# Attention with two folded feed-forward blocks: half-wide last transposes, products in 512-token blocks, and a new list of priorities

## The chip, the cores and the metric

The kernel runs on one core of one Trainium2 chip. A core has five engines with a queue each: TensorE (PE) multiplies matrices, VectorE (DVE), ScalarE (ACT) and GpSimd (POOL) work element by element, SyncE (SP) issues transfers. The metric is the device time of one execution in microseconds (us); less is better. The kernel before takes 956.4 us, the median of three runs from 956.32 to 956.83.

## The reference

```python
# q, k, v: (4, 8, 576, 64); s: (4, 8, 576); float32 throughout
scores = q @ k.T / 8
cum = cumsum(max(s, 0))
scores = where(causal, -1e9, scores + min(-(cum[i] - cum[j]), 0))
p = exp(scores - max(scores))
p = p / (sum(p) + 1e-09)
x = (p @ v).transpose(0, 2, 1, 3).reshape(2304, 512)
x = ((x @ w1) * (x @ w2)) @ w3 @ w_out     # 512 -> 1024 -> 1024 -> 512
h = x @ w_in                               # 512 -> 2048
out = (h - tanh(h)) @ w_out2               # 2048 -> 512
```

There are 32 heads (4 batches of 8), 576 tokens each.

## The kernel before

Every float32 product is made of three: a number is split into a high part (the rounded value, a cast) and a low part (the rest, a subtraction), and high x high, low x high and high x low are added up in one bank of the accumulator memory PSUM (eight banks of 128 x 512 float32, bank 58 to 65 in the orders below).

*Attention.* A head has five query tiles (64, 128, 128, 128, 128 queries). For each, PE multiplies the scores (lines 644 to 650; in batch 0, the "full" heads, one float32 product with the bias in extra rows of the operands, later two products of split operands), DVE adds the mask and takes the maximum in one pass (line 660), ACT takes the exponential with its sum (line 666). PE transposes the result e in blocks of 128 keys (`flip`, line 698), one engine copies it to SBUF as en, and PE multiplies by v for two heads together (line 730). For such a pair of heads `inverses` adds 1e-9 to the sums on DVE (line 676), takes the reciprocal (line 677), transposes it on PE (line 678), writes it to DRAM and reads it back broadcast; the result xf is multiplied by it (line 760, DVE or POOL) and split into xh and xl. Two heads give one of the four quarters k of the 512 columns of x.

*Products.* `products(j)` takes 384 tokens: for each of 8 column blocks f of w1 and w2 it adds up 4 quarters x 3 matmuls for a in bank 64, the same for b in bank 65 (line 782), copies a to SBUF (asb), multiplies b by it (line 789) and stores c. The quarters' last one can be multiplied only when the last two heads of a batch have passed the whole chain above. The weights come in as raw 64-bit pieces and are converted: absolute value on ACT (line 487), four passes on DVE (lines 488 to 493), a cast (line 389 on ACT or 390 on DVE) and a subtraction (394 or 395).

*Behind attention.* wa = w3 @ w_out, folded once (lines 838 to 840); x2 = c @ wa (lines 876 to 878); h = x2 @ w_in (line 915); g = h - tanh(h) in about ten steps over ACT, DVE and POOL (lines 923 to 930, 389, 395); out = g @ w_out2 (lines 936 to 938).

*What sets the order.* The program describes all this as operations with engines, costs, buffers and priorities. A planner (`Plan`) runs through them in its own clock, gives each engine at any time the ready operation of the least priority, and chooses the engine where an operation may go on two (`copy`, `split`, `sub`; the numbers dcopy, dsub, act, pool in `PARAM` are added to that choice). The order that comes out is emitted; each engine then runs its list in order and waits by semaphores. Where the planner expects PE to wait, up to the time `fu` of its clock, it puts in a dummy 128-wide matmul (line 546).

## Time and profile before

| | |
|---|---|
| median of three runs | 956.4 us |
| profiled execution | 956.8 us |
| its span, first to last instruction | 955.1 us |
| PE busy in the span | 942.2 us, 99% |
| DVE, ACT, POOL busy | 64%, 60%, 41% |
| mean granted PE clock | 0.998 |

PE's busy time holds the dummies too, and neighbours overlap by their tails, so a mean duration is longer than the distance between two starts. A releaser is the instruction whose end let a waiting engine go on.

### The profile page before, as it was taken

What the parts mean: (1) busy time and instruction counts of PE and PEld (TensorE: products, weight loads), DVE (VectorE), ACT (ScalarE), POOL (GpSimd) and SP (SyncE); (2) the same over time, 40 slices, a digit from 0 to 9 for tenths busy, and PEclk for the clock granted to TensorE, in tenths of its full rate; (3) what the DMA queues carried; (4) which work ended last, traced back from release to release, by engine and by line L of the source; (5) the groups of instructions that cost most, each with busy time, mean ns of one, the idle gap of its engine ahead of it and who ended that gap; (6) DMA issues with size and microseconds to landing.
All of it is one profiled execution on the core that took longest, in us unless ns stands there. A gap on an engine that the chain in (4) does not pass through costs nothing.

```text
span 955.1 us, 15454 instructions
## 1 busy us (share of the span) xinstructions
PE 942.2 (99%) x5420; PEld 810.9 (85%) x5420; DVE 611.6 (64%) x1200; ACT 568.8 (60%) x1267; POOL 393.4 (41%) x323
## 2 busy tenths in 40 slices
PE   9998999999999999999999999999999999999998
PEld 7767889998889998999888888888888888888887
DVE  6996965554443399941599859986565556655644
ACT  5885656888875454431545367766555655565565
POOL 4445865446442444220888624542222222222321
PEclk9999999999999999999999999999999999999999
DMA  6654466665441255571698731231020101000010
GB/s 207 199 172 143 132 215 195 213 217 162 141 136 48 69 201 179 204 259 53 195 347 304 250 138 67 89 110 45 1 89 1 44 1 45 23 23 1 1 45 22
DMA packets 64307, 118.96 MB, mean 125 GB/s; under 512 B 6435, under 2 KB 34323, under 8 KB 64230
## 3 DMA queue, kind: packets, MB, share of 16 engines
...
HBM read 88.81 MB, written 25.46 MB: 120 GB/s over the span
## 4 chain that ended last, share of the span: by engine, by line
PE 95%; DVE 3%; ACT 1%; issue 1%; ACTq 0%; DVEq 0%
PE bank L915 21%; PE bank L782 20%; PE bank L938 7%; PE bank L936 7%; PE bank L937 7%; PE bank L698 5%; PE bank L730 5%; PE bank L876 3%; PE bank L877 3%; PE bank L878 3%; PE bank L546 2%; PE bank L647 2%; PE bank L649 2%; PE bank L650 2%; PE bank L838 2%; PE bank L840 2%
## 5 line engine op out<-in xcount | busy, mean ns | idle before, releaser
L395 POOL TENSOR_TENSOR gl<-pg,gh 128x512 fp32r<-128x512 f32 (+1 forms) x78 | 100.2, 1284 | 254.2 <-ACT gh L389 247.5
L915 PE MATMUL bank<-x2b,wih 128*128 128x512 f32 (+1 forms) x640 | 182.6, 370 | 0.0
L915 PEld LDWEIGHTS bank<-x2b,wih 128*128 128x128 f32 x640 | 116.9, 188 | 22.1
L915 PE MATMUL bank<-x2b,wil 128*128 128x512 f32 (+1 forms) x320 | 117.9, 369 | 0.0
L938 PE MATMUL bank<-voh,gl 128*128 128x512 f32 x288 | 112.9, 392 | 0.0
L936 PE MATMUL bank<-voh,gh 128*128 128x512 f32 x288 | 112.8, 392 | 0.0
L937 PE MATMUL bank<-vol,gh 128*128 128x512 f32 x288 | 112.7, 391 | 0.0
L926 DVE TENSOR_TENSOR pg<-bank,u 128x512 f32<-128x512 f32 (+1 forms) x80 | 50.4, 631 | 90.4 <-POOL gl L395 86.3
L389 ACT ACTIVATE gh<-pg 128x512 fp32r<-128x512 f32 (+1 forms) x80 | 47.0, 588 | 99.1 <-PE bank L937 96.3
L660 DVE CUSTOM_DVE_ANT_0 e<-bank,msk 128x320 f32<-128x320 f32 (+4 forms) x160 | 65.8, 425 | 61.3 <-PE bank L650 52.1
L666 ACT ACTIVATE e<-e,nmx 128x320 f32<-128x320 f32 (+4 forms) x160 | 88.9, 556 | 21.9 <-DVE nmx L660 20.9
L929 DVE TENSOR_TENSOR th<-bank,th 128x512 f32<-128x512 f32 (+1 forms) x80 | 50.8, 635 | 45.9 <-ACT th L925 45.8
L930 DVE COPY_PREDICATED pg<-mk,th 128x512 f32<-128x512 uint32 (+1 forms) x80 | 78.2, 977 | 2.5 <-ACT mk L928 0.9
L698 PE MATMUL bank<-ident,e 128*128 128x128 f32 (+1 forms) x480 | 77.0, 276 | 1.7 <-ACT e L666 0.9
L395 POOL TENSOR_TENSOR xl<-cf,xh 128x512 fp32r<-128x512 f32 (+1 forms) x40 | 54.6, 1390 | 57.7 <-ACT xh L389 57.0
L389 ACT ACTIVATE en<-bank 64x64 f32<-64x64 f32 (+3 forms) x166 | 64.3, 407 | 16.9 <-PE bank L698 15.2
L491 DVE SCALAR_TENSOR_TENSOR wt<-wraw,wt 128x512 uint32<-128x512 uint32 x72 | 73.1, 1016 | 1.2
L789 DVE TENSOR_TENSOR cst<-bank,asb 128x384 f32<-128x384 f32 x48 | 26.6, 554 | 68.9 <-PE bank L782 52.4
L782 PE MATMUL bank<-xh,w1h 128*128 128x384 f32 x192 | 69.2, 361 | 0.1
L915 PEld LDWEIGHTS bank<-x2b,wil 128*128 128x128 f32 x320 | 60.3, 188 | 10.7
L782 PE MATMUL bank<-xh,w2h 128*128 128x384 f32 x192 | 68.3, 356 | 0.0
L928 ACT ACTIVATE mk<-u,const 128x512 f32<-128x512 f32 (+1 forms) x80 | 54.1, 676 | 19.3 <-DVE pg L930 19.0
...
## 6 DMA issues: line engine op xcount, KB each, us to landing
...
```

What stands on the lines that cost most here:

```text
L389: pl.op([("ACT", c_act(n, psum), lambda: nc.scalar.activation(dst(), src(), AF.Copy)), ("DVE", c_dve(n, not psum), lambda: nc.vector.tenso ...
L395: o.append(("POOL", c_pool2(n), lambda: nc.gpsimd.tensor_tensor(dst(), a(), b().bitcast(F32), op=ALU.subtract)))
L491: dve(lambda: nc.vector.scalar_tensor_tensor(t_.t, h32(), 0xC0000000, t_.t, op0=ALU.bitwise_and, op1=ALU.bitwise_or), 512, [r_, t_], [t_], ...
L660: nc.vector.tensor_tensor_reduce(e.t[:nq, EOFF[t] + k0:EOFF[t] + k1], bk.t[:nq, :k1 - k0], bi.t[:nq, bo + k0:bo + k1], -0.125, 3.0e38 if f ...
L666: act(lambda: nc.scalar.activation(et(), et(), AF.Exp, bias=nmx.t[:nq, i, tm:tm + 1], scale=-1.0, accum_out=ssum.t[:nq, pj, t, i:i + 1]), ...
L698: nc.tensor.transpose(bk.t[:rows, n * P:(n + 1) * P], e.t[:, EOFF[t] + c * P:EOFF[t] + c * P + rows], ident.t)
L782: nc.tensor.matmul(bk.t[:, :TB], w_.t[:, k, f * P:(f + 1) * P], x_.t[:, k, o:o + TB], start=k == 0 and i == 0, stop=k == KC - 1 and i == 2)
L915: nc.tensor.matmul(bk.t[:, :w], w_.t[:, k, a], X2.t[:, i, k, :w], start=k == 0 and n == 0, stop=k == KC - 1 and n == 2)
L930: dve(lambda pg=pg, mk=mk, th=th, c_=c_: nc.vector.copy_predicated(c_(pg), c_(mk).bitcast(U32), c_(th)), w, [mk, th], [pg], pr, two=True)
L936: nc.tensor.matmul(bank[n].t, gh.t[:, a], voh[f].t, start=f == 0, stop=False)
L937: nc.tensor.matmul(bank[n].t, gh.t[:, a], vol[f].t, start=False, stop=False)
L938: nc.tensor.matmul(bank[n].t, gl.t[:, a], voh[f].t, start=False, stop=f == NF2 - 1)
```

## The change

- *Blocks of 512 tokens.* `TB` goes from 384 to 512: four blocks of 512 and one of 256 instead of six. x lies in three buffers `xb` instead of a ring over two batches. In a block a is computed for four column blocks f, then b for the same four (four asb buffers). `products(0)` is listed right behind batch 0. All pieces of w1 are converted ahead of those of w2.
- *Heads.* Batch 1's heads aren't cut in two query groups any more (`cut`), so 16 inversions of five tiles stand where 12 of five tiles, 4 of three and 4 of two stood. The full heads have three banks for scores and four for transposes until products begin. All five tiles of the first head get their bias by a product of their own (line 661 after) instead of three, and its score product is issued without waiting for the bias. The bias is centred on the tile's first key; two of the five subtractions go to ACT.
- *Half-wide transposes.* The last key block of each query tile is transposed from 64 columns only, into the last quarter of a bank. Four matmuls of zeros at the start clear that quarter (line 553 after). The tiles e are packed and their padding isn't zeroed any more; the five blocks of the last tile are copied as 3 and 2 instead of 4 and 1.
- *The 1e-9* is added by ACT (line 687 after).
- *Absolute values* of the conversions may go to DVE (line 491 after).
- *Priorities.* Nearly all numbers in `PARAM` are new; `dcopy` from 723 to -883 (copies and casts go to DVE rather than ACT), `fu` from 215.1 to 66.7 us, the conversions' `convp` from 1692.7 to 3333.5.

By engine the emitted rows go from 1202 to 1488 on DVE, from 1109 to 792 on ACT, from 328 to 309 on POOL; dummies from 370 to 117; SP's transfers from 443 to 390.

```diff
-TB = 384
-NB = NT // TB
-RING = 2 * S
+TB = 512
+NB = (NT + TB - 1) // TB
...
-PARAM = dict(cst=1050.9, ramp0=113.5, ramp1=35.9, dsub=5134.3, dsub0=979.7, dcopy=723.0, dcopy0=29.4, dother=1000.0, dother0=1000.0, spi=1234.9, lay=4, lay0=0,
...
+PARAM = dict(cst=2849.1, ramp0=-248.5, ramp1=-108.2, dsub=6619.9, dsub0=697.3, dcopy=-883.4, dcopy0=-179.8, dother=417.2, dother0=-220.2, spi=422.3, lay=4, lay0=0,
...
-    xh, xl = (xp.buf(n, [P, KC, RING], F32R, n=KC * 4) for n in ("xh", "xl"))
+    x3 = Pool("x3", "right")
+    xb = [[p_.buf(f"{n}{i}", [P, KC, TB], F32R, n=KC * 2) for n in ("xh", "xl")] for i, p_ in enumerate((xp, xp, x3))]
...
-    asb_r = abp.ring("asb", 1, [P, TB])
+    asb_r = abp.ring("asb", 4, [P, TB])
...
-        act(lambda: nc.scalar.activation(tf(), h32().bitcast(F32), AF.Abs), 512, [r_], [t_], prio)
+        pl.op([("ACT", c_act(512), lambda: nc.scalar.activation(tf(), h32().bitcast(F32), AF.Abs)),
+               ("DVE", c_dve(512, True), lambda: nc.vector.tensor_scalar(t_.t, h32(), 0x7FFFFFFF, None, op0=ALU.bitwise_and))], r=[r_], w=[t_], prio=prio, two=True, kind="copy")
...
+    def blank(b):
+        x = msk.t[:, :D].bitcast(BF16)
+        nc.tensor.matmul(b.t[:, 3 * P:], x, x, start=True, stop=True)
+    for b in bank[3:6] + bank[7:8]:
+        pe(f_mm(P), lambda b=b: blank(b), [(msk, 0)], [b], -2900)
...
+    dve(lambda: nc.vector.tensor_scalar(neg.t[2 * NH:, :5], rel.t[2 * NH:, 0:4 * P + 1:P], -1.0, None, op0=ALU.mult), 5, [(rel, 5)], [neg], -950, fast=True)
...
+        c_ = lambda x, t=t: x[2 * NH:, t * P:t * P + 1]
+        if t % 2:
+            act(lambda a=a, o=o, t=t: nc.scalar.activation(rel.t[a:a + NH, o:o + S], rel.t[2 * NH:, :S], AF.Identity, bias=neg.t[2 * NH:, t:t + 1]), S, [(rel, 5), neg], [(rel, t)], -900 + t, extra=93.0)
+        else:
+            dve(lambda a=a, o=o, c_=c_: nc.vector.tensor_scalar(rel.t[a:a + NH, o:o + S], rel.t[2 * NH:, :S], c_(rel.t), None, op0=ALU.subtract), S, [(rel, 5), neg], [(rel, t)], -900 + t, fast=True)
...
-    s_ring = Ring(bank[0:2])
+    s_ring = Ring(bank[0:2] + bank[6:7])
     pv_ring = Ring(bank[2:3])
-    tr_ring = Ring(bank[3:3 + PARAM["ntr"]])
-    ab_ring = Ring(bank[3 + PARAM["ntr"]:])
+    tr_ring = Ring(bank[3:6] + bank[7:8])
+    ab_ring = Ring(bank[6:8])
...
-            for t0, t1 in ((3, 5),) if one else ((0, 3), (3, 5)) if 1 in groups else ((0, 3),):
+            for t0, t1 in () if one and PARAM["one"] == 5 else ((3, 5),) if one else ((0, 3), (3, 5)) if 1 in groups else ((0, 3),):
...
+                    if one and t < PARAM["one"]:
                         nc.tensor.matmul(o_, rq()[:D, q0:q1], rk()[:D, k0:k1], start=True, stop=False)
-                        nc.tensor.matmul(o_, sel(a)[:, :nq], rel.t[a:a + 1, o + k0:o + k1], start=False, stop=True)
...
-                if one and t < 3:
-                    pe(2 * f_mm4(k1 - k0), mm, [(R, 0), (rel, t), (e2[1], 4)], [bk], p_)
+                if one and t < PARAM["one"]:
+                    def bias(bk=bk, k0=k0, k1=k1):
+                        a, o = ROFF[t]
+                        nc.tensor.matmul(bk.t[:nq, :k1 - k0], sel(a)[:, :nq], rel.t[a:a + 1, o + k0:o + k1], start=False, stop=True)
+                    pe(f_mm4(k1 - k0), mm, [(R, 0)], [bk], p_ - 2000.0)
+                    pe(f_mm4(k1 - k0), bias, [(rel, t), (e2[1], 4)], [bk], p_)
...
-            dve(lambda: nc.vector.tensor_scalar(sv(), sv(), 1.0e-9, None, op0=ALU.add), n, [], [(ssum, ks)], pr + PARAM["iv"])
+            act(lambda: nc.scalar.activation(sv(), sv(), AF.Identity, bias=const.t[:, 2:3]), n, [const], [(ssum, ks)], pr + PARAM["iv"], extra=93.0)
...
-            for js in [list(range(min(4, nch)))] + ([[4]] if nch > 4 else []):
+            for js in (range(nch),) if nch < 5 else (range(3), range(3, 5)):
...
+                at = 4 - n if js[-1] == nch - 1 else 0
+                half = js[-1] == nch - 1
+
+                def tr(bk=bk, js=js, at=at):
+                    for m, c in enumerate(js):
+                        rows = D if c == nch - 1 else P
+                        nc.tensor.transpose(bk.t[:rows, (at + m) * P:(at + m + 1) * P], e.t[:, EOFF[t] + c * P:EOFF[t] + c * P + rows], ident.t)
+                pe((n - half) * f_tr() + half * f_tr(D), tr, [(e, t), ident], [bk], p_)
...
+            for j in range(b * S // TB, ((b + 1) * S - 1) // TB + 1):
+                a, z, (xh, xl), p_ = max(b * S, j * TB) - j * TB, min((b + 1) * S, (j + 1) * TB) - j * TB, xb[j % 3], c * 2 + int(b * S > j * TB)
+                o = j * TB - b * S
+                split(lambda xh=xh, a=a, z=z: xh.t[:, c, a:z], (xh, p_), lambda xl=xl, a=a, z=z: xl.t[:, c, a:z], (xl, p_), lambda a=a, z=z, o=o: X.t[:, o + a:o + z], z - a, [X], pr + PARAM["ml"])
...
+        t0, t1 = j * TB, min((j + 1) * TB, NT)
+        w = t1 - t0
+        xh, xl = xb[j % 3]
+        gs = sorted({int(b * S > t0) for b in range(B) if b * S < t1 and (b + 1) * S > t0})
+        for f0 in range(0, NF, 4):
+            asb = [asb_r.next() for _ in range(4)]
+            for m, (wh, wl) in enumerate(((w1h, w1l), (w2h, w2l))):
+                for f in range(f0, f0 + 4):
+                    pos = 1.0e6 + n_prod[0]
+                    n_prod[0] += 1
+                    bk = ab_ring.next()
+                    for k in range(KC):
+                        def mm(bk=bk, wh=wh, wl=wl, f=f, k=k):
+                            for i, (w_, x_) in enumerate(((wh, xh), (wh, xl), (wl, xh))):
+                                nc.tensor.matmul(bk.t[:, :w], w_.t[:, k, f * P:(f + 1) * P], x_.t[:, k, :w],
+                                                 start=k == 0 and i == 0, stop=k == KC - 1 and i == 2)
+                        xs = [2 * k + g for g in gs]
+                        pe(3 * f_mm(w), mm, [(xh, xs), (xl, xs), (wh, k * 2 + f // 4), (wl, k * 2 + f // 4)], [bk], pos)
+                    at = asb[f - f0]
+                    if m == 0:
+                        copy(lambda at=at: at.t[:, :w], lambda bk=bk: bk.t[:, :w], w, [bk], [at], -1e6, psum=True)
+                        continue
+                    cs = cst_r.next()
+                    dve(lambda at=at, bk=bk, cs=cs: nc.vector.tensor_tensor(cs.t[:, :w], bk.t[:, :w], at.t[:, :w], op=ALU.mult), w, [bk, at], [cs], -1e6)
+                    dma(lambda f=f, cs=cs: c_d.t[:, f, t0:t1], lambda cs=cs: cs.t[:, :w], P * w * 4, [cs], [(c_d, j)], 0)
...
+        for n in range(2 * KC):
+            src, hb, lb = ((w1, w1h, w1l), (w2, w2h, w2l))[n // KC]
+            k = n % KC
+            convert(src[k * P:(k + 1) * P, half * 512:(half + 1) * 512],
+                    lambda hb=hb, k=k, half=half: hb.t[:, k, half * 512:(half + 1) * 512], (hb, k * 2 + half),
+                    lambda lb=lb, k=k, half=half: lb.t[:, k, half * 512:(half + 1) * 512], (lb, k * 2 + half),
+                    PARAM["convp"] + half * PARAM["convq"] + n * PARAM["ramp%d" % half], None, [(rel, 4)] if half == 0 and n else [])
...
-        if h == PARAM["natb"]:
+        if h == H:
             nat.close()
+            x3.open()
+            s_ring.bufs, s_ring.i, tr_ring.bufs, tr_ring.i = bank[0:2], 0, bank[3:6], 0
         if h < H:
-            head(h, h < PARAM["natb"])
+            head(h, h < PARAM["nfull"])
+    products(0)
```

Three places of the order. The first is PE where the first products of a block wait for their last quarter of x (bank 64 and 65 hold products, 58 and 59 scores, 60 the dummies; `xh`, `xl` are the parts of x, `kh`, `qs`, `kl`, `q` those of a later head). Before:

```order
L782 MATMUL bank_64<-xh,w1h 128x384
L782 MATMUL bank_64<-xl,w1h 128x384
L782 MATMUL bank_64<-xh,w1l 128x384
L782 MATMUL bank_65<-xh,w2h 128x384
L782 MATMUL bank_65<-xl,w2h 128x384
L782 MATMUL bank_65<-xh,w2l 128x384
L649 MATMUL bank_58<-kh_112,qs_110 64x64
L650 MATMUL bank_58<-kl_114,q_116 64x64
L649 MATMUL bank_59<-kh_112,qs_110 128x192
L650 MATMUL bank_59<-kl_114,q_116 128x192
L546 LDWEIGHTS msk
L546 MATMUL bank_60<-msk 128x128
```

From here dummies and single transposes alternate up to the next product, the first of the last quarter, 256 rows further. After:

```order
L550 LDWEIGHTS msk
L550 MATMUL bank_60<-msk 128x128
L793 MATMUL bank_64<-xh_90,w1h 128x512
L793 MATMUL bank_64<-xl_91,w1h 128x512
L793 MATMUL bank_64<-xh_90,w1l 128x512
L793 MATMUL bank_65<-xh_90,w1h 128x512
L793 MATMUL bank_65<-xl_91,w1h 128x512
L793 MATMUL bank_65<-xh_90,w1l 128x512
L656 MATMUL bank_59<-kh_116,qs_114 128x192
L657 MATMUL bank_59<-kl_118,q_120 128x192
L656 MATMUL bank_58<-kh_116,qs_114 128x320
L657 MATMUL bank_58<-kl_118,q_120 128x320
```

The next product, the first of the last quarter, is row 522 of this list, and no dummy stands in between; a is begun for two column blocks (both w1h) instead of a and b for one.

The second is DVE at the inversion of the sums of heads 6 and 7, which that last quarter needs (`wt` are pieces of weights in conversion, `nmx` maxima, `e` score tiles). Before:

```order
L390 COPY en_125<-bank_62 128x4x128
L390 CAST xh<-xf_126 128x576
L676 TENSOR_SCALAR ssum<-ssum 128x10
L677 RECIPROCAL ssum<-ssum 128x10
L493 SCALAR_TENSOR_TENSOR wt_83<-wraw_105,wt_83 128x512
L489 TENSOR_SCALAR wt_88<-wt_88 128x512
L491 SCALAR_TENSOR_TENSOR wt_88<-wraw_87,wt_88 128x512
L660 ISA e_118,nmx<-bank_58,msk 64x64
```

After, the reciprocal, and further on the multiplication and the cast of the same heads' result into the last quarter:

```order
L391 CAST kh_115<-rqk_106 128x576
L497 SCALAR_TENSOR_TENSOR wt_84<-wraw_108,wt_84 128x512
L688 RECIPROCAL ssum<-ssum 128x10
L492 TENSOR_SCALAR wt_83<-wt_83 128x512
L671 ISA e_121,nmx<-bank_58,msk 64x64
L671 ISA nmx 64x1
```

```order
L493 TENSOR_SCALAR wt_89<-wt_89 128x512
L767 TENSOR_TENSOR xf_130<-xf_130,xr 128x64
L495 SCALAR_TENSOR_TENSOR wt_89<-wraw_81,wt_89 128x512
L767 TENSOR_TENSOR xf_130<-xf_130,xr 128x512
L497 SCALAR_TENSOR_TENSOR wt_89<-wraw_81,wt_89 128x512
L391 CAST xh_90<-xf_130 128x512
L391 CAST w1h<-wt_89 128x512
```

The addition has left DVE's list, and the cast of xh, which stood on ACT, follows the multiplication on DVE.

The third is PE at the last products for wa and what stands behind them (`woh`, `w3h`, `w3l`: parts of the weights). Before:

```order
L839 MATMUL bank_59<-wol,w3h_3608 128x512
L840 MATMUL bank_59<-woh,w3l_3610 128x512
L782 MATMUL bank_64<-xh,w1h 128x384
L782 MATMUL bank_64<-xl,w1h 128x384
L782 MATMUL bank_64<-xh,w1l 128x384
L782 MATMUL bank_65<-xh,w2h 128x384
L782 MATMUL bank_65<-xl,w2h 128x384
L782 MATMUL bank_65<-xh,w2l 128x384
```

After:

```order
L856 MATMUL bank_59<-wol,w3h_3213 128x512
L857 MATMUL bank_59<-woh,w3l_3215 128x512
L793 MATMUL bank_65<-xh_92,w2h 128x256
L793 MATMUL bank_65<-xl_93,w2h 128x256
L793 MATMUL bank_65<-xh_92,w2l 128x256
L793 MATMUL bank_65<-xh_92,w2h 128x256
L793 MATMUL bank_65<-xl_93,w2h 128x256
```

Behind this place stand 240 products of a and b before, 384 wide, and 108 after, most of them 256 wide.

## Rows read from the trace of the kernel before

**Rows 1.** the page's first part: engine, busy us (share of the span), instructions

```profile
PE 942.2 (99%) x5420; PEld 810.9 (85%) x5420; DVE 611.6 (64%) x1200; ACT 568.8 (60%) x1267; POOL 393.4 (41%) x323
```

**Rows 2.** stretches: length, busy us PE, PEld, DVE, ACT, POOL, clock, DMA

```profile
0.00:97.00 97.00, 89.72 (x801) 71.24 (x802) 76.44 (x230) 68.06 (x192) 45.66 (x46) 0.98 0.60 179
118.00:320.00 202.00, 201.95 (x1477) 182.71 (x1476) 94.92 (x338) 145.47 (x417) 97.59 (x87) 1.00 0.52 160
340.00:400.00 60.00, 60.00 (x295) 53.13 (x294) 58.67 (x87) 28.24 (x48) 24.91 (x18) 1.00 0.52 179
```

**Rows 3.** the same of line 546 alone: length, PE, PEld, clock, DMA

```profile
0.00:97.00 97.00, 30.11 (x370) 26.66 (x370) 0.98 0.60 179
```

**Rows 4.** timeline of PE: start, us, instruction, [idle before, releaser]

```profile
74.39 0.67 PE L546 MATMUL bank<-msk 128*128 128x128 bf16 x9
...
87.16 0.27 PE L678 MATMUL bank<-ident,ssum 128*6 128x128 f32 x1 [2.85 <-DVE ssum L677]
...
88.38 1.91 PE L546 MATMUL bank<-msk 128*128 128x128 bf16 x16
...
95.58 0.42 PE L782 MATMUL bank<-xh,w1h 128*128 128x384 f32 x1
```

**Rows 5.** timeline of DVE

```profile
71.83 2.15 DVE L676 TENSOR_SCALAR ssum<-ssum 128x10 f32<-128x10 f32 x1
...
83.66 3.13 DVE L676 TENSOR_SCALAR ssum<-ssum 128x6 f32<-128x6 f32 x1 [0.34 <-ACT e L666]
```

**Rows 6.** timeline of POOL

```profile
85.50 1.26 POOL L760 TENSOR_TENSOR xf<-xf,xr 128x512 f32<-128x512 f32 x1
```

**Rows 7.** timeline of ACT

```profile
92.04 0.44 ACT L389 ACTIVATE xf<-bank 128x320 f32<-128x320 f32 x1 [2.01 <-PE bank L730]
...
92.84 0.67 ACT L389 ACTIVATE xh<-xf 128x576 fp32r<-128x576 f32 x1
```

**Rows 8.** lines of DVE, 0 to 71 us: count, busy us, mean ns

```profile
L660 DVE CUSTOM_DVE_ANT_0 e<-bank,msk 128x192 f32<-128x192 f32 (+4 forms) x40 | 16.4, 424 | 7.9 <-PE bank L645 4.6 <-PE bank L647 2.9
L491 DVE SCALAR_TENSOR_TENSOR wt<-wraw,wt 128x512 uint32<-128x512 uint32 x11 | 9.4, 851 | 0.0
L493 DVE SCALAR_TENSOR_TENSOR wt<-wraw,wt 128x512 uint32<-128x512 uint32 x10 | 7.7, 767 | 0.0
L488 DVE TENSOR_SCALAR wt<-wt 128x512 f32<-128x512 f32 x12 | 6.4, 543 | 0.2
L489 DVE TENSOR_SCALAR wt<-wt 128x512 uint32<-128x512 uint32 x11 | 5.1, 459 | 0.0
```

**Rows 9.** stretches of PE: line 782 at 420, others

```profile
420.00:440.00 20.00, 20.00 (x118) 20.00 (x117) 1.00 0.41 131
...
543.00:548.00 5.00, 5.00 (x44) 1.00 0.80 290
...
700.00:720.00 20.00, 20.00 (x90) 1.00 0.30 106
```

**Rows 10.** lines of PE by shape: the two transpositions

```profile
L698 PE MATMUL bank<-ident,e 128*128 128x128 f32 x416 | 64.6, 276 | 1.7 <-ACT e L666 0.9 <-ACT rinv L389 0.6
...
L698 PE MATMUL bank<-ident,e 128*64 128x128 f32 x64 | 16.5, 275 | 0.0
```

**Rows 11.** stretches behind the idle time at 84 to 87 us

```profile
88.00:90.00 2.00, 2.00 (x19) 1.94 (x17) 0.51 (x1) 1.47 (x4) 0.86 (x1) 0.50 0.23 52
90.00:92.00 2.00, 2.00 (x17) 1.10 (x15) 0.00 (x0) 0.03 (x1) 0.00 (x0) 0.66 0.02 3
```

**Rows 12.** lines of DVE, 340 to 400 us

```profile
L491 DVE SCALAR_TENSOR_TENSOR wt<-wraw,wt 128x512 uint32<-128x512 uint32 x18 | 19.7, 1094 | 0.4
```

**Rows 13.** spread of a line: ns least, median, most, first and last start

```profile
L838 PE MATMUL bank<-woh,w3h x64: 389/393/402, 349.0 to 413.1; 128*128 128x512 f32 x64
...
L782 PE MATMUL bank<-xh,w1h x192: 332/336/448, 48.2 to 453.1; 128*128 128x384 f32 x192
```

**Rows 14.** the same of line 676

```profile
L676 DVE TENSOR_SCALAR ssum<-ssum x20: 156/222/3130, 24.1 to 300.2; 128x10 f32<-128x10 f32 x12, 128x6 f32<-128x6 f32 x4, 128x4 f32<-128x4 f32 x4
```

More of the change, by code (lines that the diff above doesn't have):

```diff
@@ L121 @@
     WINDOW = 3413.0
+    PHASE = 1000.0
     fill_until, fill_from = 0.0, 0.0
@@ L255, in order @@
             if got.xfer is not None:
-                late = LAND[3 if pipe > t + LAND[0] else 2]
+                late = LAND[3 if pipe > t + LAND[0] else 2] - (1000.0 if t < 100.0 else 0.0)
                 pipe = max(pipe, t + LAND[0]) + got.xfer
@@ L290, in f_mm4, with f_pair @@
     return 2 * [(112.0 if m > 64 else 58.0, 0.8333 * n + 3.5)]
-def f_pair(n):
-    return 2 * [(112.0, 0.8333 * n + 8.0)]
+def f_pair(ns):
+    f = [(112.0, 0.8333 * n + 3.5) for n in ns for _ in range(2)]
+    return [(f[0][0], f[0][1] + 100.0)] + f[1:-1] + [(f[-1][0], f[-1][1] + 100.0)]
 def f_tr(n=P):
@@ L441, in tile_kernel @@
     q2 = [p_.buf(f"q2{i}", [P, S], F32R, n=3) for i, p_ in enumerate((att, att))]
-    e2 = [att.buf(f"e{i}", [P, 1856], n=5) for i in range(PARAM["ne"])]
+    e2 = [att.buf(f"e{i}", [P, 1600], n=5) for i in range(PARAM["ne"])]
     nmx = att.buf("nmx", [P, 2, 6], n=12)
@@ L559, in tile_kernel @@
         if e is None:
-            for x in en:
-                zero([later(x, EB + 1024, ETOT, low), later(x, 0, D, low)], [P, D], [x], 30, r=scan)
             zero([lambda: ssum.t], [20], [ssum], -5, 1.0)
@@ L650, in mm @@
                         nc.tensor.matmul(o_, Q2.t[:NR, q0:q1], KL.t[:NR, k0:k1], start=False, stop=True)
-                if one and t < 3:
-                    pe(2 * f_mm4(k1 - k0), mm, [(R, 0), (rel, t), (e2[1], 4)], [bk], p_)
+                if one and t < PARAM["one"]:
[4 more added lines that the diff above has]
+                    pe(f_mm4(k1 - k0), bias, [(rel, t), (e2[1], 4)], [bk], p_)
                 elif full:
@@ new lines, in flip @@
+                o = (q0 if t < 3 else EB + q0 - 320) + 256 * js[0]
+                if n == 1:
+                    view = lambda d, o=o: d.t[:, o:o + nq]
+                    src = lambda bk=bk, at=at: bk.t[:, at * P:at * P + nq]
+                else:
+                    sh = P if o + 256 * n > ETOT else 0
+                    view = lambda d, n=n, o=o, sh=sh: d.t[:, o - sh:o - sh + 256 * n].rearrange("p (c q) -> p c q", q=256)[:, :, sh:sh + nq]
+                    src = lambda bk=bk, n=n, at=at: bk.t[:, at * P:(at + n) * P].rearrange("p (c q) -> p c q", q=P)
@@ L722, in pv @@
                 q0, n, parts = 320, 256, [3, 4]
-                lst = [(c, EB + c * 256, 256) for c in range(3)] + [(3, EB + 832, 192), (4, EB + 1088, 64)]
+                lst = [(c, EB + c * 256, 256) for c in range(3)] + [(3, EB + 832, 192), (4, EB + 1216, 64)]
             X = xf[(h // 2) % 2]
@@ L731, in mm @@
                                          start=j == 0, stop=j == len(lst) - 1, skip_group_check=True)
-            pe([y for x in lst for y in f_pair(x[2])], mm, V2 + [(en[k], parts) for k in range(2)], [bk], p_)
+            pe(f_pair([x[2] for x in lst]), mm, V2 + [(en[k], parts) for k in range(2)], [bk], p_)
             copy(lambda: X.t[:, q0:q0 + n], lambda: bk.t[:, :n], n, [bk], [X], p_, psum=True)
@@ L792, in tile_kernel @@
-    for half in range(2):
-        for k in range(KC):
-            for src, hb, lb in ((w1, w1h, w1l), (w2, w2h, w2l)):
-                convert(src[k * P:(k + 1) * P, half * 512:(half + 1) * 512],
-                        lambda hb=hb, k=k, half=half: hb.t[:, k, half * 512:(half + 1) * 512], (hb, k * 2 + half),
-                        lambda lb=lb, k=k, half=half: lb.t[:, k, half * 512:(half + 1) * 512], (lb, k * 2 + half),
-                        PARAM["convp"] + half * PARAM["convq"] + (2 * k + (src is w2)) * PARAM["ramp%d" % half], PARAM["rawp"] if half == 0 and 2 * k + (src is w2) < PARAM["raw0"] else None,
-                        [(rel, 4)] if half == 0 and 2 * k + (src is w2) else [])
+        t0, t1 = j * TB, min((j + 1) * TB, NT)
@@ L811, in tile_kernel @@
             gate = Buf()
-            pl.op([("X", 0.0, lambda: None)], r=[(xh, [4 * k + 2 + g for k in range(KC) for g in range(2)])], w=[gate])
+            pl.op([("X", 0.0, lambda: None)], r=[xb[1][0]], w=[gate])
         if b == B - 1:
+            x3.close()
             att.close()
@@ L817, in tile_kernel @@
         for j in range(NB):
-            if b * S < (j + 1) * TB <= (b + 1) * S or b == 1 and (j + 1) * TB <= S:
+            if b * S < min((j + 1) * TB, NT) <= (b + 1) * S:
                 products(j)
@@ L879, in tile_kernel @@
                 parts = range(n * 4, n * 4 + 4)
-                ps = [4 * c + 2 * n + g for c in range(KC) for g in range(2)]
-                pe(12 * f_mm(n_), mm, [(xh, ps), (xl, ps), (wah, parts), (wal, parts)], [bks[d]], 1.2e6 + j * 100 + n * 10 + d)
+                pe(12 * f_mm(n_), mm, xb[n] + [(wah, parts), (wal, parts)], [bks[d]], 1.2e6 + j * 100 + n * 10 + d)
         for d in range(KC):
```

85 lines of the change are left out of this document (19 added, 66 removed).

## The prediction

> **What bounds the kernel now.** I read the busy shares first, then the stretches, then the waits. TensorE (PE) is busy 942.2 of 955.1 us [rows 1], so only PE's own work, or its few gaps, can give much. But the share counts the dummy matmuls of line 546 as work. By stretches [rows 2] PE is full from 118 us on (201.95 of 202.00 up to 320), and nearly every gap lies ahead: up to 97 us it is busy for 89.72, so 7.3 are idle, and 30.11 of the busy time are 370 dummies [rows 3]. Overlap of neighbours is in that figure: 9 dummies in a row take 0.67 us [rows 4], 0.055 each if the last one's tail is left out, and 16 at the lower clock 1.91, 0.11 each; with some 70 of the 370 at that clock they are about 25 us. Until the first product a, b over the fourth quarter of x (k=3) starts at 95.58 [rows 4], PE has stood or idled through about 25 + 6 = 31 us.
>
> Why there: k=3 needs heads 6 and 7. Followed back [rows 4 to 7]: on VectorE (DVE) the 1e-9 addition of these heads runs from 71.83 to 73.98, then come the reciprocal and its transposition on PE. The reciprocals go through DRAM and back; GpSimd (POOL) multiplies until 86.76. The cast of x then waits for ScalarE (ACT), which stands in line 389 for the matmuls of later heads (2.01 us) and casts only at 92.84; POOL takes the low part from there, and k=3 starts. The same line 676 again holds DVE for 3.13 us at 83.66 [rows 5], and PE waits 2.85 us for it at 87.16 [rows 4].
>
> **The change part by part.**
>
> *The 1e-9 addition on ACT, casts on DVE, the first weights alone.* In the new order the fourth reciprocal has less work ahead of it on DVE. I price rows ahead of it by means of the first 71 us [rows 8]: a weight conversion is 0.543 + 0.459 + 0.851 + 0.767 = 2.62 us, and about one and a half fewer stand ahead (-3.9); three additions of 0.22 [rows 14] and the one of 2.15 go (-2.8); memsets of the padded score tiles go (-0.2, a guess). So the reciprocal comes 6.9 us earlier, near 67. Behind it, DVE has twelve softmax pieces (0.424 each, with 0.08 for reading the maximum 6.0), about one and two thirds conversions (4.4), and two multiplications, a subtraction, a copy and two casts (some 0.5 each, 3), 13.4 us by such prices, up to the cast of x, which now stands on DVE right behind its multiplication and no longer behind ACT's wait: 92.84 - 86.76 = 6.1 us go. Start of k=3: 95.6 - 6.9 - 6.1 = 82.6; DVE's own sum, 67 + 13.4 and about 1.5 for the low part on POOL, gives 82 too. Bounds: 0 to -13.0; I take -13.0, because both waits are named by rows and both lose their cause in the order.
>
> *Work that is put ahead of k=3.* By the order the new list has more of it: 18 products 512 wide instead of 384 (18 x 0.056 = 1.0), 12 more transpositions at 0.11 (1.3), four pairs of score products 288 wide and three 448 wide (14 matmuls at 0.44 ns a column, 2.2), three own bias products of the first head (0.9). That is 5.4 us moved out of the full stretch into gaps: -5.4, but the three bias products are new: +0.9. Bounds -5.4 to 0 (if the gaps are where this work isn't ready).
>
> *512-token blocks.* 1152 matmuls 384 wide become 768 of 512 and 192 of 256. A stretch of pure 384 holds 118 in 20 us, one of 512 holds 90, one of 256 holds 44 in 5 us [rows 9]; two in each lie half outside by their tails, so 0.1724, 0.2273 and 0.119 apart: 1152 x 0.1724 = 198.6 against 768 x 0.2273 + 192 x 0.119 = 197.4, so -1.2. One matmul more or less at an edge moves it by 2: bounds -4 to +1. Issuing a for four columns before b only changes which bank is copied when.
>
> *Half-wide transposes.* 320 full and 160 half ones stand where 416 and 64 stood. A full one lasts 276 ns, a half one 275 [rows 10]: nothing, 0 to -1. Four transpositions of sums fall away with the halved heads of batch 1: 4 x 0.11 = -0.4. The four blanking matmuls at the start run while PE has nothing else.
>
> *The dummies end at 66.7 instead of 215 us in the planner's clock.* 117 remain. Where PE then waits, its clock can fall. Row: after the idle time of 2.85 us before 87.16 the granted clock was 0.50 and 0.66 of full in 88 to 92 [rows 11], the level of 1.2 GHz and then a mix with 2.4; 4 us at 0.58 lost 1.7 of work. Three such dips instead of one would cost 5.0: I take +1.3 over before, bounds -1.7 to +5.
>
> The Trainium skill ("TensorE: Matmul & The Clock Gate", What's actually happening) says that the throttled state is the default and activity releases it; the trace agrees with those 0.50 and 0.66 after an idle 2.9 us, and by that rule fewer dummies speak against this change.
>
> *Copies and casts on DVE.* DVE gets 1488 rows instead of 1202, ACT 792 instead of 1109. By mean durations DVE's load rises from 601 to about 729 us, ACT's falls by 150. In 118 to 320 DVE was busy 94.92 of 202 [rows 2], so this mostly fits. In batches 1 and 2 I get about 61 and 64 us of DVE work against 69 and 59 of PE work: PE may wait now and then for a softmax. I take +2, bounds 0 to +10.
>
> *The end.* Behind the last h there were 45 matmuls of out, now 24: 24 x 0.2273 = 5.5 us cover the last tanh chain instead of 10.2. If that isn't enough PE waits: +0.5, bounds 0 to the 4.8 that went.
>
> Sum against the profiled execution's 956.8: -13.0 - 5.4 + 0.9 - 1.2 - 0.4 + 1.3 + 2 + 0.5 = -15.3, so 941.5; the median of the runs lies 0.4 below that execution: 941.1.
>
> **The rivals.**
>
> *The start of k=3 doesn't move.* For it: the chain still goes through DRAM, and DVE, now with the casts, is busy 76.44 of 97 us already [rows 2]. Then the first -13.0 goes, the work ahead still fills gaps: -5.4 + 0.9 - 1.2 - 0.4 + 1.3 + 2 + 0.5 = -2.3, 954.1, with two more dips of the clock 957. Against it: the long additions of line 676 and ACT's wait are plain in rows.
>
> *All gaps vanish.* The new order keeps 117 dummies, 7 us, and the planner counted on hardly any idle time besides. Then the 31 us fall to 7, with the terms of DVE, the clock and the end at nothing: 956.4 - 24 + 0.9 - 1.2 - 0.4 = 931.7. Against it: waits of 1 to 3 us between engines that no plan foresaw, in the kernel before as well.
>
> *Slower: DVE becomes the bound at the wa stage.* In 340 to 400 us DVE was busy 58.67 of 60 [rows 2] with the conversions of w3 and w_out, whose dearest pass takes 1.094 us there instead of 0.851 [rows 12, 8]. PE was not late, because products a, b filled in: the last wa started at 413.1 and the last a, b at 453.1 [rows 13]. By the new order 108 products (mostly 256 wide, 13 us) stand behind the last wa instead of 240 (40 us). If PE gets through the same work 15.3 us earlier, at 437.8, the last wa is due at 425: a slack of 12 us against 413. DVE's extra 128 us fall partly ahead of it; if 30 us of them push the conversions, wa ends at 443, 18 late: 941 + 18 = 959. It decides from 12 us on, and is slower than before from 27 on. Against it: DVE had 107 us free in 118 to 320.
>
> The Trainium skill ("SBUF — State Buffer", Who interferes with whom) says that DVE and GpSimd share a pair of ports that one holds for a whole instruction while the other stands, and that copies and casts in DVE's fast mode take it; PE and ACT aren't touched. The trace agrees as far as it goes: an addition of a median 0.22 us took 3.13 at most [rows 14] and ended with POOL's multiplication [rows 6]. By that rule the casts moved to DVE lengthen beside POOL, as that addition did.
>
> *The clock.* Without dummies PE might stay at the lower level through much of 60 to 82 us: 22 x 0.42 = 9 us lost instead of 1.3, so 949 or so.
>
> **How the numbers follow.** Forecast 0.55 (own range 933 to 950); no earlier start 0.20 (952 to 958, of which 0.13 faster, 0.05 the same, 0.02 slower); all gaps vanish 0.10; DVE late 0.10; the clock 0.05. A difference under 0.2% (1.9 us) can't be told from none here. Faster 0.55 + 0.13 + 0.10 + 0.05 = 0.83, same 0.05, slower 0.12. For 8 in 10 the range goes from 928, under the vanished gaps, to 956, most of the case in which k=3 doesn't move; beyond are DVE's case and the rest of that one.
>
> **What would show it.** Right: first matmul of k=3 near 82; PE idle and dummies up to 97 us together about 15 instead of 31; the short addition on ACT under 0.3 us and PE's wait for the transposition of sums gone; a, b at 0.227 apart; no idle PE in front of wa. Wrong: k=3 after 90; the clock under 0.9 between 60 and 97; PE waiting on DVE for softmax pieces between 120 and 300 by more than 10 us; idle time between the last a, b and the next stage.

## The result, and the profile after

The changed kernel takes 940.32 us (median of four runs, 937.82 to 941.51) against 956.62 (four runs, 956.32 to 956.93): a ratio of 0.9826, 95% interval 0.9806 to 0.9846. The profiled execution is the fastest of the four, 937.8 us with a span of 936.1; what made the others slower is seen in the second trace of the same kernel below.

The page's line of busy times, and the stretches of [rows 2] and [rows 3] again (length, busy us of PE, PEld, DVE, ACT, POOL, clock, DMA; the last row is line 550 alone, the dummies, with PE and PEld):

```profile
PE 929.3 (99%) x4981; PEld 764.3 (82%) x4981; DVE 704.9 (75%) x1486; ACT 412.6 (44%) x950; POOL 368.6 (39%) x304
...
0.00:97.00 97.00, 94.69 (x678) 72.73 (x678) 78.93 (x249) 82.29 (x241) 45.51 (x45) 0.96 0.74 210
118.00:320.00 202.00, 202.00 (x1275) 164.93 (x1274) 142.61 (x424) 79.57 (x238) 80.29 (x73) 1.00 0.43 131
340.00:400.00 60.00, 60.00 (x263) 48.95 (x262) 56.50 (x103) 8.52 (x14) 22.14 (x16) 1.00 0.50 166
...
0.00:97.00 97.00, 10.46 (x117) 9.47 (x117) 0.96 0.74 210
```

Up to 97 us PE now idles 2.3 instead of 7.3 us, and dummies take 10.5 instead of 30.1 of its busy time. That is the whole change: summed by the distance from each matmul's start to the next one's, the dummies (with the four blanking matmuls) fell from 24.9 to 9.5 us and idle time from 8.1 to 1.9, 21.6 together, while scores with their bias products took 1.9 more, h 1.5 more, and the other kinds stayed within 0.8 (products a, b 210.4 before, 210.1 after). DVE's extra 93 us of work cost PE one wait of 0.6 us.

The chain of heads 6 and 7, against [rows 5 to 7] and the last of [rows 4], in the timelines of ACT, DVE, POOL and PE:

```profile
64.21 0.29 ACT L687 ACTIVATE ssum<-ssum,const 128x10 f32<-128x10 f32 x1
64.53 0.22 DVE L688 RECIPROCAL ssum<-ssum 128x10 f32<-128x10 f32 x1 [0.72 <-ACT ssum L687]
78.81 0.68 DVE L767 TENSOR_TENSOR xf<-xf,xr 128x512 f32<-128x512 f32 x1
80.01 0.41 DVE L391 CAST xh<-xf 128x512 fp32r<-128x512 f32 x1
80.51 1.40 POOL L396 TENSOR_TENSOR xl<-xf,xh 128x512 fp32r<-128x512 f32 x1 [2.65 <-PE bank L712]
82.05 0.48 PE L793 MATMUL bank<-xh,w1h 128*128 128x512 f32 x1
```

The addition takes 0.29 us, the reciprocal stands at 64.5 instead of 74.0, the cast follows its multiplication by half a microsecond instead of six, and k=3 starts at 82.05 instead of 95.58.

One thing got worse. Stretches of PE alone, 8 to 18 us, and what it did there:

```profile
8.00:10.00 2.00, 2.00 (x6) 1.00 0.68 238
10.00:12.00 2.00, 2.00 (x6) 0.71 0.95 170
12.00:14.00 2.00, 2.00 (x6) 0.50 0.96 353
14.00:16.00 2.00, 2.00 (x13) 0.50 0.67 181
16.00:18.00 2.00, 2.00 (x24) 0.58 0.63 174
...
9.03 1.01 PE L661 MATMUL bank<-rel,e 1*128 1x448 f32 x2
9.98 1.47 PE L652 MATMUL bank<-rqk 64*128 64x288 f32 x4
11.38 2.28 PE L661 MATMUL bank<-rel,e 1*128 1x288 f32 x4
```

The granted clock falls to 0.50 (1.2 GHz) though PE is busy every moment: with the first head's score products (64 rows) and bias products (one row), which follow each other without dummies. The low stretch lasts from 10.9 to 17.7 us. In [rows 11] the clock had fallen after idle time. In the kernel before it read 1.00 from 6 to 20 us, with 36 dummies in a row among such products.

### The profile page after: what moved, and what is told of

It is laid out like the page before. It is cut to its first block, busy times and chain, and to the rows that moved or that the text cites. A ratio compares the mean times of both kernels' runs of the same rounds, so it can differ in the third digit from the quotient of the medians.

```text
span 936.1 us, 14400 instructions
## 1 busy us (share of the span) xinstructions
PE 929.3 (99%) x4981; PEld 764.3 (82%) x4981; DVE 704.9 (75%) x1486; ACT 412.6 (44%) x950; POOL 368.6 (39%) x304
## 4 chain that ended last, share of the span: by engine, by line
PE 94%; DMA 3%; DVE 1%; ACT 1%; issue 0%; POOL 0%; SPq 0%; DVEq 0%; ACTq 0%
PE bank L930 21%; PE bank L793 20%; PE bank L953 7%; PE bank L951 7%; PE bank L952 7%; PE bank L712 5%; PE bank L739 5%; PE bank L894 4%; PE bank L892 4%; PE bank L893 4%; PE bank L656 2%; PE bank L657 2%; PE bank L857 1%; PE bank L855 1%; PE bank L856 1%; PE bank L654 1%
## 5 line engine op out<-in xcount | busy, mean ns | idle before, releaser
L938 ACT ACTIVATE u<-bank 128x512 f32<-128x512 f32 (+1 forms) x80 | 44.5, 556 | 179.5 <-PE bank L930 164.3
L677 ACT ACTIVATE e<-e,nmx 64x64 f32<-64x64 f32 (+4 forms) x160 | 89.1, 558 | 48.5 <-DVE nmx L671 47.9
L671 DVE CUSTOM_DVE_ANT_0 e<-bank,msk 128x192 f32<-128x192 f32 (+4 forms) x160 | 65.0, 424 | 22.5 <-PE bank L657 16.0
L942 DVE SCALAR_TENSOR_TENSOR pg<-sq,pg 128x512 f32<-128x512 f32 (+1 forms) x80 | 72.7, 909 | 0.1
L490 ACT ACTIVATE wt<-wraw 128x512 f32<-128x512 f32 x46 | 31.0, 674 | 90.1 <-DMA wraw<-w3t 45.5
L953 PEld LDWEIGHTS bank<-voh,gl 128*128 128x128 f32 x288 | 54.0, 188 | 11.9
L793 PE MATMUL bank<-xh,w2h 128*128 128x512 f32 (+1 forms) x160 | 63.1, 394 | 0.6 <-DVE asb L391 0.6
L952 PEld LDWEIGHTS bank<-vol,gh 128*128 128x128 f32 x288 | 54.1, 188 | 11.5
L951 PEld LDWEIGHTS bank<-voh,gh 128*128 128x128 f32 x288 | 54.2, 188 | 11.2
L793 PE MATMUL bank<-xh,w1h 128*128 128x512 f32 (+1 forms) x160 | 63.1, 394 | 0.0
```

Source lines behind the costliest of these rows:

```text
L671: nc.vector.tensor_tensor_reduce(e.t[:nq, EOFF[t] + k0:EOFF[t] + k1], bk.t[:nq, :k1 - k0], bi.t[:nq, bo + k0:bo + k1], -0.125, 3.0e38 if f ...
L677: act(lambda: nc.scalar.activation(et(), et(), AF.Exp, bias=nmx.t[:nq, i, tm:tm + 1], scale=-1.0, accum_out=ssum.t[:nq, pj, t, i:i + 1]), ...
L793: nc.tensor.matmul(bk.t[:, :w], w_.t[:, k, f * P:(f + 1) * P], x_.t[:, k, :w], start=k == 0 and i == 0, stop=k == KC - 1 and i == 2)
L942: dve(lambda sq=sq, pg=pg, c_=c_: nc.vector.scalar_tensor_tensor(c_(pg), c_(sq), SQ_K, c_(pg), op0=ALU.add, op1=ALU.mult), w, [sq, pg], [p ...
L951: nc.tensor.matmul(bank[n].t, gh.t[:, a], voh[f].t, start=f == 0, stop=False)
L952: nc.tensor.matmul(bank[n].t, gh.t[:, a], vol[f].t, start=False, stop=False)
```

## The experiments

The theory at the start: the gain is PE time up to 97 us that now has work in it, led by the earlier start of k=3. Most edits make the planner list everything anew, so that each kernel differs in more than its diff; the traces are read for where. The kernel before was run again beside the experiments; its medians were 956.9, 956.6 and 956.0 us, and each ratio is taken against its own.

**The addition on DVE again.** `act(... AF.Identity, bias=const.t[:, 2:3] ...)` back to `dve(... tensor_scalar(sv(), sv(), 1.0e-9 ...))`.

> The changed kernel with the 1e-9 added by DVE again (one line back; the list is planned anew and holds 153 dummies instead of 117). Theory (the gain is early PE time that now has work in it, whatever engine adds): about 2 us of dummies come back, 942 to 943 us. Rival (the long additions on DVE were the main cause of the early gaps): four of them of 2 to 3 us each hold the reciprocals up again, k=3 after 88 us, 947 us or more.

948.08 us (ratio to the kernel before 0.9912, 0.9895 to 0.9928): the rival's number, though no addition took its 2 to 3 us; the longest is that of heads 6 and 7 with 1.38. The reciprocal came at 70.10, k=3 at 92.3. And the list moved more than the addition: it gave the cast of x to ACT as well. The multiplication and the cast of heads 6 and 7, in the timelines of DVE and ACT:

```profile
86.57 0.63 DVE L767 TENSOR_TENSOR xf<-xf,xr 128x512 f32<-128x512 f32 x1
88.25 0.61 ACT L390 ACTIVATE xh<-xf 128x512 fp32r<-128x512 f32 x1
```

The multiplication ends 7.7 us later than in the changed kernel, and from there to k=3 it takes 5.1 us instead of 2.6. The clock was low for 10.2 us too, longer than in the trace above (6.8). So the 7.8 us aren't the addition's alone.

**Copies on ACT again.** `dcopy=-883.4, dcopy0=-179.8` to `723.0, 29.4`.

> The changed kernel with the old numbers dcopy and dcopy0, so that copies and casts go to ACT again (DVE 1146 rows, ACT 1143; 131 dummies). Theory: the cast of x falls back behind ACT's waits, k=3 starts 3 to 6 us later, but PE has other work meanwhile; 942 to 945 us. Rival (casts on DVE lengthen beside POOL and cost the change time): faster than the changed kernel by 2 us or more, 938 or less. Rival (the freed ACT queue is the main gain): 948 or more.

947.92 us (0.9913, 0.9898 to 0.9927), 2.9 above the theory's range and at the bound of the second rival. The cast of x on ACT came at 86.6 and k=3 at 90.5, 8.4 us later and not 3 to 6. But the reciprocal came late too, at 70.46 instead of 64.53 although the addition is still on ACT, and the multiplication ended at 84.6 instead of 79.5; so this list doesn't show the cast alone either. The low clock lasted 10.2 us. (This trace reads 0.95 where the others read 1.00, though h takes 200.1 us by distances as in them; its 0.93 in the table below is that level and no dip.) The rival by which casts on DVE cost time is not borne out: with them on ACT it is 7.6 us slower.

**Three bias products.** `one=5` to `one=3`.

> The changed kernel in which only three tiles of the first head have their own bias product, as before; the two others wait for the transfer of the bias. The new list holds 222 dummies instead of 117. Theory: 105 dummies more are 6 us, less up to 3 us for the dip of the clock at 10 to 17 us, which the products of one row bring and dummies between them prevent: 943 to 947 us. Rival (the start doesn't matter, since heads 6 and 7 set when the products begin): 940 to 941.

944.72 us (0.9878, 0.9863 to 0.9892), as the theory has it: k=3 at 89.3, and the granted clock 1.00 up to 120 us, with 17 dummies behind the third bias product and 32 more up to 12.3 us.

**The numbers without the code.** The new `PARAM` values, wherever the kernel before has the name, in its own code.

> The kernel before with all numbers of the changed kernel's table and none of its code: 261 dummies instead of 370. Theory (numbers and code each bring work into the early gaps): 109 dummies less are 6 us, and casts go to DVE: 948 to 952 us. Rival (the numbers are all): 942 or less. Rival (the numbers fit only the new code): 956 or more.

964.97 us: slower than before (1.0087, 1.0072 to 1.0102), as the last rival has it. k=3 started at 89.1, and the 13 us that were lost lie at 447 to 461 us, where the first matmuls of x2 wait: 3.9 us for ACT's cast and 9.2 for POOL's subtraction (why, under "The addition on ACT alone").

**Dummies among the first head's products.** Four behind each of its 14 products, in the same operation.

> The changed kernel with four dummy matmuls behind each score product and each bias product of the first head (56 in all; the list holds 169 dummies instead of 117). Theory (in the changed kernel the clock falls to 0.50 at 10.8 to 17.3 us although PE is never idle there, because the first head's products of 64 rows and of one row don't hold it; dummies between them do): granted clock 1.00 from 10 to 20 us, and 2 to 4 us faster than the changed kernel, 936 to 938 us. Rival (the clock falls for what came before 5 us, or dummies only delay the head's products): the dip stays, 940 to 943 us.

947.24 us (0.9909, 0.9892 to 0.9925). Wrong: the clock read 1.00 to 15.3 us and then was low to 29.0 (0.55 from 20 to 30 us), though about a third of PE's time among these products went to dummies, and k=3 came at 97.0.

**a and b in turn.** `for f0 in range(NF)` with one asb buffer each, and w1, w2 converted in turn.

> The changed kernel in which a and b alternate by column block again, and the pieces of w1 and w2 are converted in turn. Theory (a ahead of b makes products of w1 alone ready early; 18 products of w1 stand ahead of the last quarter of x): with b's weights late, fewer products are ready before 82 us; 2 to 5 us slower than the changed kernel, 942 to 945 us. Rival (heads 6 and 7 alone decide): 940 to 941.

947.51 us (0.9905, 0.989 to 0.992), above both ranges. k=3 at 85.5, within those of the changed kernel's two traces (82.1 and, below, 86.0); the low clock lasts 10.2 us, and behind 545 us PE waits 4.2 us for DVE. So it doesn't tell what the order of a and b is worth.

**Blocks of 384 tokens** in the changed kernel: `TB = 384`, x buffers 512 wide, buffer (0, 1, 2, 0, 1, 0)[j].

> The changed kernel with products in six blocks of 384 tokens instead of four of 512 and one of 256 (1152 matmuls instead of 960, three x buffers as in the changed kernel). Theory (the block width is worth 1.2 us by the distances of starts, and a little early work): 941 to 944 us. Rival (the saving of the change is the wider blocks): 950 or more.

960.65 us (1.0046, 1.0031 to 1.0061), the rival's side, but not for its reason: products a, b took 210.9 us by distances against 210.1. The time went into k=3 at 91.0, 8.7 us of waiting where x2 begins (445 to 454 us) and the low clock (9.5 to 19.8, and again behind that wait, 449.8 to 460.1 us).

**Banks not lent.** `s_ring = Ring(bank[0:2])`, `tr_ring = Ring(bank[3:6])`.

> The changed kernel in which the heads of batch 0 have two banks for scores and three for transposes all along, the products' two banks are not lent. The list holds 154 dummies. Theory: 37 dummies more are 2 us, and softmax pieces wait for banks at times: 942 to 945 us. Rival (banks don't limit): 940 to 941.

951.09 us (0.9942, 0.9925 to 0.9958); more than expected. The trace is of the slowest of the six executions, 955.2 us; k=3 started at 107.4 in it. The two bias products of 448 columns take 1.86 us here against 1.01 above: PE runs at half speed up to about 27 us (28 dummies at 23.0 still take 3.19), though this trace's clock reads 1.00 throughout. So a reading of 1.00 in the first microseconds of a trace needs such a check; in the other traces, too, the dummies up to 4 to 7 us are 0.11 us apart under a reading of 1.00. What the banks are worth without this isn't shown.

**The changed kernel again.**

> The changed kernel once more, unchanged, for its spread and a second trace. Theory (its runs differ because the dip of the clock in the first 20 us is longer or shorter from run to run): 938 to 942 us, and this trace, if its time differs by 1 us or more from the first one's 937.8, shows a dip of another length or place between 5 and 25 us and the same waits of PE otherwise. Rival (the spread comes from transfers or from waits later on): the dip is the same, and idle time of PE differs behind 25 us.

940.49 us (five runs, 938.55 to 942.43; ratio 0.9831, 0.9819 to 0.9844). The profiled run took 942.4, 4.6 more than the first trace's. Stretches of PE alone, and two rows of its timeline:

```profile
6.00:8.00 2.00, 2.00 (x10) 1.00 1.08 386
8.00:10.00 2.00, 2.00 (x5) 0.61 0.39 129
10.00:12.00 2.00, 2.00 (x3) 0.50 0.94 188
...
20.00:22.00 2.00, 2.00 (x17) 0.50 0.04 14
22.00:24.00 2.00, 2.00 (x28) 0.97 1.00 302
...
8.26 1.71 PE L652 MATMUL bank<-rqk 64*128 64x448 f32 x2
23.22 2.06 PE L654 MATMUL bank<-rqk 69*128 69x64 f32 x8
```

The same list, but the clock falls at 8.5 instead of 10.9 us and comes back at 22.1 instead of 17.7 (one expectation above has 17.3, which is wrong). The same eight products of line 654 start at 23.22 instead of 19.78, 3.44 us later, and k=3 at 86.02 instead of 82.05; PE's idle time is the same within half a microsecond. So between these two executions most of the 4.6 us is the length of that dip. The mean clocks of the changed kernel's nine runs fit: 0.996 at 937.8 and 938.6 us, 0.994 at 940.2 to 941.5, 0.993 at 941.2 and 942.4.

**Twenty-four dummies in a run** behind the third bias product.

> The changed kernel with 24 dummy matmuls in one run behind the third bias product of the first head; the list moves them there from later places (122 dummies instead of 117). Theory (a run of dummies over a microsecond long holds the clock, as the 36 in a row at 9.4 us of the kernel before did, where four at a time did not): granted clock 1.00 up to 25 us; the softmax of the last two tiles begins 1.3 us later, PE's work there goes at twice the speed: 938 to 941 us, runs within 1.5 us of each other. Rival (the dip comes whatever stands there): a dip between 8 and 25 us again, 941 to 944 us.

946.96 us (0.9904, 0.9882 to 0.9925), runs from 942.8 to 950.2. Wrong: the clock reads 1.00 to 14 us and then PE is slow to 28:

```profile
12.00:14.00 2.00, 2.00 (x10) 1.00 0.94 352
14.00:16.00 2.00, 1.85 (x14) 0.56 0.70 223
16.00:18.00 2.00, 2.00 (x6) 0.50 0.88 231
...
24.00:26.00 2.00, 2.00 (x9) 0.50 0.34 95
26.00:28.00 2.00, 2.00 (x13) 0.53 0.19 60
...
15.97 3.97 PE L654 MATMUL bank<-rqk 69*128 69x64 f32 x8
```

The dip moved, and the new list has taken the 46 dummies away that stood at 15.7 to 19.8 us, where the changed kernel's clock came back. Here it came back at 27.9, behind transposes and products with v and without dummies. What would keep it high without losing more is open.

**The addition on ACT alone**, in the kernel before.

> The kernel before with the 1e-9 added by ACT, alone (343 dummies instead of 370). Theory (the long additions held the reciprocals up, but ACT's wait in front of the cast of x stays): the reciprocal of heads 6 and 7 comes 2 to 3 us earlier, the products over the last quarter of x start 1 to 3 us earlier than 95.6: 953 to 956 us. Rival (what the first experiment showed, nearly 8 us, is the addition by itself): 949 or less.

963.16 us: slower (1.0073, 1.006 to 1.0086), which neither expected. The reciprocal comes 2.6 us earlier (71.38), the cast waits 2.0 us behind the multiplication instead of 6.1, and k=3 starts at 90.0, 5.5 us earlier than before; more than that is lost at the start of x2. PE's waits, SP's queue there (start, us, transfer), and the spread of the last products of a, b and of the last wa (last figure of each: start of the last one):

```profile
PE bank L876 <- ACT xh L389: 7.1, 1, 7.1
PE bank L877 <- POOL xl L395: 4.2, 1, 4.2
...
425.09 12.80 SPq L386 DMA_DIRECT2D c_d<-cst  x4
446.46 0.33 SPq L386 DMA_DIRECT2D wraw<-w_in  x1
446.85 1.85 SPq L386 DMA_DIRECT2D vol<-wt_d  x4
448.81 2.99 SPq L386 DMA_DIRECT2D cf<-c_d  x5
...
L782 PE MATMUL bank<-xh,w2l x192: 332/336/343, 48.7 to 436.6; 128*128 128x384 f32 x192
L838 PE MATMUL bank<-woh,w3h x64: 389/389/402, 339.9 to 447.0; 128*128 128x512 f32 x64
```

The first loads of c stand behind a load of w_in that goes out only when a conversion has freed its buffer at 446.46. But the last matmul for wa starts at 447.43, and c's buffers take the memory of wa's parts (`wtmp` closes, then `cp` opens): in all 14 traces the first load of c goes out 0.2 to 1.4 us behind the start of that last matmul. The difference is what still stands behind it on PE:

| kernel | last a, b | last wa | first load of c | first x2 | products a, b behind the last wa |
|---|---|---|---|---|---|
| before | 455.6 | 413.6 | 413.9 | 455.7 | 240 |
| changed | 434.8 | 421.0 | 421.8 | 435.0 | 108 |
| before, new numbers | 438.9 | 447.1 | 447.3 | 451.3 | 0 |
| blocks of 384 | 438.9 | 444.4 | 444.6 | 450.8 | 0 |
| before, addition on ACT | 436.6 | 447.4 | 448.8 | 454.9 | 0 |

In the three slow lists nothing covers the load, the cast and the subtraction of c. The wait has an aftermath: the clock falls to 0.50 in it and stays there for a while (here from 450.8 to 464.5 us), and x2's matmuls take 102.0 us by distances instead of 98.6. In the changed kernel five of these loads are issued in time:

```profile
421.81 0.43 SPq L387 DMA_DIRECT2D cf<-c_d  x1
422.29 0.45 SPq L387 DMA_DIRECT2D c_d<-cst  x1
422.79 2.40 SPq L387 DMA_DIRECT2D cf<-c_d  x4
```

**Fewer dummies alone**, in the kernel before: `fu=66693`.

> The kernel before with dummies only up to 66.7 us of the planner's clock, alone (239 instead of 370). Theory (dummies stand where PE waits anyway): no gain, 956 to 958 us, and the granted clock lower between 66 and 100 us than before, up to 3 us slower. Rival (dummies push real work back): 131 fewer are 7 us, 950 or less.

955.38 us (0.9993, 0.9984 to 1.0002): no difference, as the theory has it, 0.6 below its range. From 80 to 90 us PE is busy 5.47 us and the clock 0.66, where before it was 7.15 and 0.90; k=3 starts at 94.3. These 131 dummies covered waiting and cost nothing; taking them away gains nothing.

All kernels side by side; idle time of PE is the stretch less its busy time, from one trace each, which needn't be that of the median (that of the changed kernel is the fastest of its four, that of the banks the slowest of its six):

| kernel | median us | k=3 starts | dummies | PE idle 0 to 120 | 120 to 545 | clock 10 to 20, 20 to 30 |
|---|---|---|---|---|---|---|
| before | 956.0 | 95.6 | 370 | 9.1 | 0.1 | 1.00, 1.00 |
| changed | 940.3 | 82.1 | 117 | 2.3 | 0.6 | 0.66, 1.00 |
| changed, again | 940.5 | 86.0 | 117 | 2.3 | 0.9 | 0.50, 0.89 |
| addition on DVE | 948.1 | 92.3 | 153 | 3.5 | 1.1 | 0.51, 0.98 |
| copies on ACT | 947.9 | 90.5 | 131 | 3.4 | 2.4 | 0.51, 0.93 |
| three bias products | 944.7 | 89.3 | 222 | 5.1 | 0.5 | 1.00, 1.00 |
| four dummies each | 947.2 | 97.0 | 169 | 3.6 | 0.2 | 0.77, 0.55 |
| a, b in turn | 947.5 | 85.5 | 117 | 3.0 | 0.2 | 0.52, 1.00 |
| blocks of 384 | 960.7 | 91.0 | 134 | 3.2 | 10.8 | 0.51, 1.00 |
| banks not lent | 951.1 | 107.4 | 154 | 5.2 | 0.4 | not shown |
| 24 dummies in a run | 947.0 | 93.1 | 122 | 3.4 | 1.3 | 0.71, 0.61 |
| before, new numbers | 965.0 | 89.1 | 261 | 7.3 | 13.3 | 1.00, 1.00 |
| before, addition on ACT | 963.2 | 90.0 | 343 | 4.9 | 11.5 | 1.00, 1.00 |
| before, fewer dummies | 955.4 | 94.3 | 239 | 11.3 | 0.5 | 1.00, 1.00 |

## Why the prediction was right

The measured 940.3 lies 0.8 below the forecast 941.1, and the mechanism is the one forecast: work in place of early gaps, with k=3 earlier. That the number fits so closely is in part luck, since several terms were off and made up for each other. Profile against profile the sum gave 15.3 us; the first trace shows 19.0, the second 14.4.

*The start of k=3*: 82.6 was forecast, 82.05 and 86.0 are measured. The reciprocal came even earlier than 67, at 64.5, but from there to the cast DVE took 15.5 us instead of 13.4; the two errors cancel. What each of the two causes is worth isn't shown: with the addition back on DVE the cast went to ACT too, with the copies back on ACT the reciprocal was late too, and both starts fell back to 90 or later. The addition alone, in the kernel before, moved k=3 by 5.5. The Trainium skill ("SBUF — State Buffer", Who interferes with whom) says that ACT never waits for the ports which DVE and GpSimd share; here the addition took 0.287 to 0.307 us on ACT in all 16 cases, against 0.156 to 3.130 on DVE [rows 14].

*The work ahead of it*: 13.0 + 5.4 were forecast for both steps; PE's dummies and idle time fell by 21.6. Up to 97 us some 12 us of them are left, where about 15 were forecast. The step was undersized by 3, of which 1.8 lie behind k=3, where hardly a gap was left (idle 97 to 118 us: 1.8 before, none after). Lending the products' banks has no term in the prediction; the list without it was 10.8 us slower, which is more than either part of the chain, though its trace isn't comparable.

*512-token blocks*: -1.2 was wrong in size. A stretch of products 512 wide holds 88 in 20 us here, 0.233 apart in the median, not the 90 of h and out from which I took 0.2273:

```profile
300.00:320.00 20.00, 20.00 (x88) 1.00 0.12 43
```

Products took 210.1 us against 210.4: 0.3, no gain to speak of. Both are 12 to 13 us above my 198.6 and 197.4: in the kernel before products were 0.173 apart from 420 to 440 us, where I read them, but 0.191 in the mean from 118 to 320, among other work.

*Half-wide transposes*: nothing, as forecast; 278 and 276 ns:

```profile
L712 PE MATMUL bank<-ident,e 128*128 128x128 f32 x320 | 58.9, 278 | 0.6 <-ACT e L677 0.6
...
L712 PE MATMUL bank<-ident,e 128*64 128x128 f32 x160 | 41.9, 276 | 0.0
```

*The clock*: its size (+1.3) was near in the first trace alone, its place wrong. I looked for dips where PE waits from 60 to 97 us; the clock is 1.00 there. It falls at 11 us, with PE busy. In the first trace the low clock lasts 6.8 us, in the second 13.7, against 3.4 before; at half speed that is 1.7 and 5.1 us more lost than before, by estimate from these lengths. The step that failed is that only idle time was taken to let the clock fall.

*DVE* (+2): 0.6 us, one wait for a copy of a at the end of the products. DVE's load rose by 93 us, not by 128, and it had the room that [rows 2] showed. The slower rival's place was right and its slack was there: the last wa started at 420.5 instead of 413.1, forecast as due by 425; products a, b ran on to 434.8, and no wait for wa came:

```profile
L855 PE MATMUL bank<-woh,w3h x64: 389/389/400, 355.8 to 420.5; 128*128 128x512 f32 x64
...
PE bank L793 <- DVE asb L391: 0.6, 1, 0.6
PE bank L712 <- ACT e L677: 0.6, 2, 0.4
PE bank L656 <- DVE nmx L671: 0.5, 1, 0.5
```

Three of the other lists did go past 958 us at this very place, by the rival's price and only in part by its cause. The last wa started at 444 to 447 us, with no product of a and b left behind it to cover the load of c. From 400 to 440 us DVE was full in one of them (38.1 of 40 us, blocks of 384), but not in the others (20.4 and 11.0). No wait of PE for wa is named in any of the three; the list had put it last, and why the planner did so isn't shown. It is the point at which this change could have become slower.

*The end* (+0.5): no wait is named there. Instead h takes 1.5 us more (889 distances within h are 208.8 ns in the mean instead of 207.1); why is open. It goes with the new code and not with its numbers: 200.1 to 200.2 us in nine of the ten traces of it, 201.9 in the tenth, whose clock falls within h ("a and b in turn"), against 198.5 to 198.7 in the four of the kernel before's code.

What each part is worth by itself stays open too, because every edit brought another list. The dip doesn't explain the differences, though. In the traces with the addition on DVE, the copies on ACT and a, b in turn it lasts 10.2 us, less than the 13.7 of the changed kernel's second trace, and yet they take 946.7, 949.5 and 947.7 us against 942.4, so at least some 4, 7 and 5 us are not the dip's. The list with three bias products costs more than the 4.4 us between the medians: its dummies and idle time are 8.8 us above those of the changed kernel's first trace, and part of this comes back because its trace has no dip.
